# Score blocks of 64 keys, two heads to a fill, and PV in 64x32 tiles, in a fused attention and gated-MLP kernel

## The chip, the cores and the metric

The program runs on one core of a Trainium2 chip. The metric is the device time of one execution in microseconds (us), the median of several runs. TensorE is called PE in the profile, VectorE DVE, ScalarE ACT, GpSimd POOL.

## The reference, cut to what matters

Sequence 2048, width 512, 32 heads of 16, four segments of 512 tokens. Each segment has causal softmax attention within itself (`a_dot`), mixed with a linear-attention memory of the earlier segments (`a_mem`), and a gated MLP runs beside it:

```python
logits = einsum('bhqd,bhkd->bhqk', qs, ks) * scale + mask      # causal, 512 x 512 per head and segment
p = softmax(logits)
a_dot = einsum('bhqk,bhkd->bhqd', p, vs)
...
o = g * a_mem + (1.0 - g) * a_dot                              # then o @ wo
...
gate = gate * (gate > 0)                                       # gate, up: x times 512 x 1792 weights
h = gate * up                                                  # then h @ W_down
...
return g * a + (1 - g) * b                                     # a: attention, b: MLP, g: a gate per token
```

The matter here is the causal triangle. Scores are computed transposed, keys on the partitions and queries along the row. A block of keys needs only the queries from its first key on, so small key blocks waste less of the triangle.

## The kernel before: the parts that matter

One *unit* is 8 heads of one segment (16 units). A *fill* is one use of the score tile `S` (four PSUM banks, 4 x 512 columns): four row groups of TensorE make the scores of four heads at once, ScalarE takes the exponential of all 128 x 2048 into a tile `E`, and GpSimd zeroes the triangle at the diagonal blocks. *PV* then multiplies E by V, four heads side by side in 128x32 tiles. `G` names the other four PSUM banks, one for each other product of TensorE; a bank is free again when ScalarE or VectorE has copied or used its content (an *evacuation*). phi(Q) and phi(K) are the feature maps that the linear-attention memory takes.

```python
# unit(i): 5 fills of 128-key blocks; (key block, head parity, column offset, width)
FL = [[(0, 0, 0, 512)], [(1, 0, 0, 384), (3, 0, 384, 128)], [(2, 0, 0, 256), (2, 1, 256, 256)],
      [(0, 1, 0, 512)], [(1, 1, 0, 384), (3, 1, 384, 128)]]
...
b = op(f"e{s}{c}.{n}", {"ACT": 1.88}, f, deps=[a], ...)                   # exp
for o in offs:                                                            # mask
    v = eb_.t[:, :, o:o + P]
    nc.gpsimd.affine_select(out=v, in_=v, ..., pattern=[[0, 4], [1, P]], channel_multiplier=-1)
m = op(f"m{s}{c}.{n}", {"POOL": 0.7 * len(offs)}, f, deps=[b], ...)
...
# PV of one head parity r, placed behind fill 1 of the next unit
for kb, src, off, w in ((0, ea, 0, 512), (1, ebf, 0, 384), (2, ec, 256 * r, 256), (3, ebf, 384, 128)):
    for j in range(4):
        nc.tensor.matmul(g.t[32 * j:32 * j + 32, L - w:L], lhsT=Vp[s].t[:, kb, h * HP:h * HP + 32],
                         rhs=src.t[:, j, off:off + w], ..., tile_position=(0, 32 * j))
```

Even heads take their 16 rows of K straight from `KT`; odd heads take 32 rows of `KO`, a copy of K with the even heads' rows set to zero (a GpSimd operation).

Everything above is called `op(name, {engine: price}, ...)`. It isn't executed in the order of the source: the kernel has a list scheduler in Python that runs when the program is built. It walks a model of the five engines in which each operation takes its *price* in us, and writes the instructions of each engine in the order that the model found.

The softmax here doesn't subtract the row's maximum and nothing guards it: scores larger than these inputs give would overflow.

Of the kernel before, what the change touches and what calls it, by code (L numbers as in the profile page):

```python
# [8 lines left out]
F32 = mybir.dt.float32  # L9
# [16 lines left out]
VW = H * HP + 16  # L26

# [25 lines left out]
class Sched:  # L53
# [20 lines left out]
    def run(self):  # L74
# [14 lines left out]
        while len(order) < n:  # L89
            best = None  # L90
            for e, lst in cand.items():
                ests = []
                for o in lst:
                    t = max(free[e], o.ready)
                    ok = True
                    for b in o.alloc:
                        fr = b.pool.free
                        if not fr:
                            ok = False
                            break  # L100
                        t = max(t, min(fr)[0])
                    if ok:
                        ests.append((t, o))
                if not ests:
                    continue
                t0 = min(t for t, _ in ests)
                if e == "PE":
                    def pk(x):
                        t, o = x
                        k = o.key  # L110
                        if o.mode == "C":
                            k += 4.0 if mode == "D" else -20.0
                        elif o.mode == "D" and mode == "C" and not o.flex:
                            k += 3.0
                        return (k, o.seq)
                    pick = min((x for x in ests if x[0] <= t0 + 0.02), key=pk)
                else:
                    pick = min((x for x in ests if x[0] <= t0 + 0.02), key=lambda x: (x[1].cls, x[1].key, x[1].seq))
                t, o = pick
                if best is None or (t, o.cls, o.key) < best[0]:  # L120
                    best = ((t, o.cls, o.key), o, e, t)
# [37 lines left out]
def kernel(  # L159
# [36 lines left out]
    mcol = tl("mcol", [P, 1], F32)  # L196
    bdm = tl("bdm", [P, 8, DH], F32)
# [3 lines left out]
    xTp = pool("xT", 3, [P, NC, L])  # L201
    xnp = pool("xn", 1, [P, 4, D])
    hTp = pool("hT", 22, [P, L])
    QTp, KTp, KOp = pool("QT", 6, [P, L]), pool("KT", 6, [P, L]), pool("KO", 6, [P, L])
    pqp = pool("pq", 5, [P, L])
# [3 lines left out]
    Vpp = pool("Vp", 2, [P, 4, VW])  # L209
    Ep = pool("E", 7, [P, 4, L])  # L210
    Tp = pool("T", 3, [P, 2, 16, 32], F32)
# [40 lines left out]
    def c_warm(e):  # L252
        nc.scalar.activation(mcol[:], zero[:, 0:1], ACT.Exp)  # L253
    o_warm = op("warm", {"ACT": 1.5}, c_warm, deps=[o_zero], cls=0, key=-100)

    def c_mcol(e):
        nc.vector.memset(mcol[:], 1.0)
        for j in range(4):
            nc.vector.memset(mcol[32 * j:32 * j + 16, :], 0.0)
    o_mcol = op("mcol", {"DVE": 0.4}, c_mcol, deps=[o_warm], key=-50)  # L260

    def c_vones(e):
        for t in Vpp.tiles:
            nc.gpsimd.memset(t[:].rearrange("p a b -> p (a b)"), 1.0)
    o_vones = op("vones", {"POOL": 4.0}, c_vones, key=-60)
# [217 lines left out]
    o_q, o_k, o_ko, o_pq, o_v = {}, {}, {}, {}, {}  # L483
# [52 lines left out]
    def proj_k(s, c):  # L536
        g, k, ko = Buf(G), Buf(KTp), Buf(KOp)
        KT[s, c], KO[s, c] = k, ko
# [5 lines left out]
        def f(e):  # L544
            (nc.vector if e == "DVE" else nc.gpsimd).tensor_scalar(ko.t[:], k.t[:], mcol[:, 0:1], None, ALU.mult)  # L545
        o_ko[s, c] = op(f"ko{s}{c}", {"DVE": 0.45} if s == 0 and c < 2 else {"POOL": 0.8}, f, deps=[b, o_mcol], key=a.key, cls=1, alloc=[ko], uses=[k])
# [12 lines left out]
    def proj_v(s, t):  # L559
        g = Buf(G)  # L560
        if t == 0:
# [9 lines left out]
                       uses=[g, Vp[s]])  # L571

# [99 lines left out]

    def unit(i):
        s, c = units[i]
        k0 = TA0 + i * PU
        FL = [[(0, 0, 0, 512)], [(1, 0, 0, 384), (3, 0, 384, 128)], [(2, 0, 0, 256), (2, 1, 256, 256)],
              [(0, 1, 0, 512)], [(1, 1, 0, 384), (3, 1, 384, 128)]]
        E, masks = [], []
        for n, parts in enumerate(FL):
            sp, eb_ = Buf(Spool), Buf(Ep)  # L680
            kf = k0 + n * PU / 5

            def f(e, parts=parts, sp=sp):
                for kb, r, off, w in parts:
                    for j in range(4):
                        q0 = L - w
                        if r == 0:
                            rows = slice(32 * j, 32 * j + 16)
                            ks = KT[s, c].t
                        else:  # L690
                            rows = slice(32 * j, 32 * j + 32)
                            ks = KO[s, c].t
                        nc.tensor.matmul(sp.t[:, j, off:off + w], lhsT=ks[rows, kb * P:(kb + 1) * P],  # L693
                                         rhs=QT[s, c].t[rows, q0:L], start=True, stop=True,
                                         tile_position=(32 * j, 0))
            a = op(f"f{s}{c}.{n}", {"PE": MM}, f,
                   deps=[o_q[s, c], o_k[s, c] if all(p[1] == 0 for p in parts) else o_ko[s, c],
                         (fill_prev[0], 0.0) if fill_prev[0] else None],
                   key=kf, mode="R", alloc=[sp], uses=[QT[s, c], KT[s, c], KO[s, c]])
# [10 lines left out]
            def f(e, eb_=eb_, offs=offs):  # L710
                for o in offs:
                    v = eb_.t[:, :, o:o + P]
                    nc.gpsimd.affine_select(out=v, in_=v, compare_op=ALU.is_ge, fill=0.0, base=0,  # L713
                                            pattern=[[0, 4], [1, P]], channel_multiplier=-1)
            m = op(f"m{s}{c}.{n}", {"POOL": 0.7 * len(offs)}, f, deps=[b], key=kf, uses=[eb_])
            E.append(eb_)
            masks.append(m)
        pending[0] = (i, E, masks)
# [5 lines left out]
    def dens(s, k0, org):  # L724
# [12 lines left out]
        def f(e):  # L737
            nc.vector.transpose(T.t[:, 0, :, :].rearrange("p b e -> p (b e)"), g.t[:])
        a = op(f"trd{s}", {"DVE": 0.72}, f, deps=[a], key=k0, cls=0, alloc=[T], uses=[g])

        def f(e):
            nc.gpsimd.tensor_scalar(CMD[:, 0], T.t[:, 0, :, 0:8], 1e-6, None, ALU.add)
# [25 lines left out]
    def rest(i, E, masks, behind):  # L768
        s, c = units[i]
        k0 = TA0 + i * PU  # L770
        pvs = []
        for r in range(2):
            g = Buf(G)
            ea, ebf, ec = E[3 * r], E[3 * r + 1], E[2]

            def f(e, r=r, g=g, ea=ea, ebf=ebf, ec=ec):
                for kb, src, off, w in ((0, ea, 0, 512), (1, ebf, 0, 384), (2, ec, 256 * r, 256), (3, ebf, 384, 128)):
                    for j in range(4):
                        h = 8 * c + 2 * j + r
                        nc.tensor.matmul(g.t[32 * j:32 * j + 32, L - w:L],  # L780
                                         lhsT=Vp[s].t[:, kb, h * HP:h * HP + 32],
                                         rhs=src.t[:, j, off:off + w],
                                         start=(kb == 0), stop=(kb == 3), tile_position=(0, 32 * j))
            a = op(f"pv{s}{c}.{r}", {"PE": 0.57}, f,
                   deps=[masks[3 * r], masks[3 * r + 1], masks[2]] + [o_v[s, t] for t in range(4)] +
                   ([(pvs[0][0], 0.0)] if r else [(behind, 0.0)] if behind else []),
                   key=k0 - 100, mode="C", alloc=[g], uses=[ea, ebf, ec, Vp[s]])
            pvs.append((a, g))
# [19 lines left out]
        for kind, lst in ((0, pvs), (1, recs)):  # L808
            if not lst:
                continue  # L810
            T, O = Buf(Tp), Buf(Op_)
            tr = []
            for r, (a, g) in enumerate(lst):
                def f(e, T=T, g=g, r=r):
                    nc.vector.transpose(T.t[:, r, :, :].rearrange("p b e -> p (b e)"), g.t[:])  # L815
                tr.append(op(f"tr{s}{c}.{kind}{r}", {"DVE": 0.72}, f, deps=[a] + tr, key=k0 + PU * 0.8, cls=0,
                             alloc=[T] if r == 0 else [], uses=[g] + ([] if r == 0 else [T])))
            if kind == 0:
                sm = Buf(smp)

                def f(e, T=T, sm=sm):
                    nc.vector.reciprocal(sm.t[:], T.t[:, :, :, DH])
                    nc.vector.tensor_tensor(sm.t[:], sm.t[:], RG[s % 2][:, c, :, :], ALU.mult)
                a = op(f"cf{s}{c}", {"DVE": 0.55}, f, deps=tr + [org], key=k0 + PU, alloc=[sm], uses=[T])

                def f(e, T=T, sm=sm, O=O):
                    nc.vector.tensor_tensor(O.t[:].rearrange("p b r e -> p r b e"), T.t[:, :, :, 0:DH],
                                            sm.t[:][:, :, :, None].to_broadcast([P, 2, 16, DH]), ALU.mult)
                a = op(f"pr{s}{c}.0", {"DVE": 0.80}, f, deps=[a], key=k0 + PU, alloc=[O], uses=[T, sm])
            else:  # L830
                cm = CM[s]

                def f(e, T=T, cm=cm, O=O):
                    nc.vector.tensor_tensor(O.t[:], T.t[:, 0, :, :].rearrange("p b (r e) -> p b r e", r=2),
                                            cm.t[:, c, :, :, None].to_broadcast([P, 16, 2, DH]), ALU.mult)
                a = op(f"pr{s}{c}.1", {"DVE": 0.80}, f, deps=tr + o_cm[s, c], key=k0 + PU, alloc=[O], uses=[T, cm])
# [4 lines left out]
        deps = [outs[0][0]]  # L841
        if s > 0:
# [4 lines left out]
            deps = [op(f"ad{s}{c}", {"DVE": 0.5} if (s, c) == (NSEG - 1, NC - 1) else {"POOL": 0.8}, f, deps=[outs[0][0], outs[1][0]], key=k0 + PU, uses=[Oa, Ob])]  # L847
# [92 lines left out]
```

## Time and profile before

| | before |
|---|---|
| median | 272.53 us (272.49 to 272.73) |
| TensorE busy | 265.1 of 270.6 us |
| ScalarE, VectorE, GpSimd busy | 209.5, 175.1, 169.0 us |
| granted TensorE clock | 1.00 |

Lines of the page of the kernel before: the busy times, the busy share of GpSimd and the granted clock in 40 equal slices of the span (tenths), and the shares of the chain of waits, followed back from the last instruction.

```profile
PE 265.1 (98%) x2650; PEld 117.2 (43%) x2650; DVE 175.1 (65%) x345; ACT 209.5 (77%) x200; POOL 169.0 (62%) x319
...
POOL 8095889983598892795439963678585352633500
PEclk9999999999999999999999999999999999999999
...
PE 93%; DVE 3%; ACT 1%; ACTq 1%; issue 0%; DVEq 0%
```

The chain is TensorE from end to end, and GpSimd has light slices (2 to 6) between the full ones. The chain in order of time, around the first PV (start in us, length in us, engine, tile, line, matmuls):

```profile
30.84 0.33 PE S L693 x8
31.17 1.20 PE G L780 x32
32.37 1.73 PE G L236 x32
34.10 0.33 PE S L693 x8
34.43 2.70 PE G L238 x12
```

A fill (L693) lasts 0.33 us and streams 512 columns, which at the dense rate is 0.216 us; the other 0.11 us is the change of tiling. PV (L780) is 1.20 us. The dense work behind it (L236, in PV's tiling) runs 8 matmuls' worth of columns in 1.73 us, 0.216 each, with no change of tiling in between. In this profile there are 165 blocks, that is, stretches of matmuls in one tiling.

Two groups of GpSimd (busy us, mean ns of one, idle time before and what ended it):

```profile
L713 POOL TENSOR_SCALAR_AFFINE_SELECT E<-E 128x512 bf16<-128x512 bf16 x128 | 87.5, 703 | 68.0 <-ACT E L706 64.1
L545 POOL TENSOR_SCALAR KO<-KT,mcol 128x512 bf16<-128x512 bf16 x14 | 23.3, 1672 | 9.2 <-ACT KT L503 6.9
```

The masks wait for ScalarE (64.1 us of GpSimd's idle time), so GpSimd is early. Note the 1672 ns of the masked K: the schedule prices it at 0.8 us.

### The profile page before, as it was taken

What the parts mean: (1) busy time and instruction counts of PE and PEld (TensorE: products, weight loads), DVE (VectorE), ACT (ScalarE), POOL (GpSimd) and SP (SyncE); (2) the same over time, 40 slices, a digit from 0 to 9 for tenths busy, and PEclk for the clock granted to TensorE, in tenths of its full rate; (3) what the DMA queues carried; (4) which work ended last, traced back from release to release, by engine and by line L of the source; (5) the groups of instructions that cost most, each with busy time, mean ns of one, the idle gap of its engine ahead of it and who ended that gap; (6) DMA issues with size and microseconds to landing.
All of it is one profiled execution on the core that took longest, in us unless ns stands there. A gap on an engine that the chain in (4) does not pass through costs nothing.

```text
span 270.6 us, 6534 instructions
## 1 busy us (share of the span) xinstructions
PE 265.1 (98%) x2650; PEld 117.2 (43%) x2650; DVE 175.1 (65%) x345; ACT 209.5 (77%) x200; POOL 169.0 (62%) x319
## 2 busy tenths in 40 slices
PE   8999999999999999999999999999999999999995
PEld 6444444434443444434344444343344444434454
DVE  1499978978893454798777543789865432748251
ACT  3599889989977688989996868898878677887511
POOL 8095889983598892795439963678585352633500
PEclk9999999999999999999999999999999999999999
DMA  6998993024400100001001000000000000000002
GB/s 177 282 236 219 321 284 100 0 41 101 95 2 21 41 21 2 0 0 22 19 2 40 33 28 22 1 2 0 2 4 0 22 19 23 20 0 2 2 8 72
DMA packets 27597, 15.49 MB, mean 57 GB/s; under 512 B 13616, under 2 KB 27568, under 8 KB 27568
## 3 DMA queue, kind: packets, MB, share of 16 engines
q1 hardware_dynamic: 26736, 14.63, 21.5%
q10 hardware_dynamic: 832, 0.46, 0.6%
q8 instruction: 20, 0.33, 0.5%
q14 instruction: 9, 0.07, 0.1%
HBM read 9.84 MB, written 2.10 MB: 44 GB/s over the span
## 4 chain that ended last, share of the span: by engine, by line
PE 93%; DVE 3%; ACT 1%; ACTq 1%; issue 0%; DVEq 0%
PE G L238 61%; PE G L236 13%; PE S L693 10%; PE G L780 7%; PE S L396 2%; PE G L578 1%; DVE QT L501 1%; DVE pq L531 1%; DVE pq L530 0%; DVE KT L501 0%; ACT L253 0%; ACT QT L503 0%; PE G L730 0%; ACTq L304 0%; DVE T L815 0%
## 5 line engine op out<-in xcount | busy, mean ns | idle before, releaser
L706 ACT ACTIVATE E<-S 128x2048 bf16<-128x2048 f32 x80 | 150.0, 1875 | 25.5 <-PE S L693 22.0
L713 POOL TENSOR_SCALAR_AFFINE_SELECT E<-E 128x512 bf16<-128x512 bf16 x128 | 87.5, 703 | 68.0 <-ACT E L706 64.1
L618 DVE TENSOR_TENSOR hT<-G,rg 128x512 bf16<-128x512 f32 x56 | 37.6, 679 | 23.0 <-ACT rg L614 17.5
L238 PE MATMUL G<-xT,wu_sb 128*128 128x512 bf16 x194 | 51.0, 380 | 0.0
L238 PE MATMUL G<-xT,wg_sb 128*128 128x512 bf16 x184 | 48.7, 380 | 0.1
L815 DVE STREAM_TRANSPOSE T<-G 128x512 f32<-128x512 f32 x44 | 29.6, 698 | 17.6 <-PE G L780 16.5
L238 PE MATMUL G<-wd_sb,hT 128*128 128x512 bf16 x166 | 40.4, 380 | 0.1
L614 ACT ACTIVATE rg<-G 128x512 bf16<-128x512 f32 x56 | 32.5, 596 | 6.1 <-PE G L236 2.8
L545 POOL TENSOR_SCALAR KO<-KT,mcol 128x512 bf16<-128x512 bf16 x14 | 23.3, 1672 | 9.2 <-ACT KT L503 6.9
L238 PEld LDWEIGHTS <-wu_sb 128*128 128x128 bf16 x194 | 17.7, 98 | 22.6 <-issue 3.5
L238 PEld LDWEIGHTS <-wg_sb 128*128 128x128 bf16 x184 | 16.6, 98 | 21.2 <-issue 4.0
L238 PEld LDWEIGHTS <-hT 128*128 128x128 bf16 x166 | 14.9, 98 | 19.0 <-issue 3.8
L780 PE MATMUL G<-E,Vp 128*32 128x256 bf16 (+3 forms) x512 | 20.5, 301 | 0.0
L657 ACT ACTIVATE os<-G,ngcol 128x512 bf16<-128x512 f32 x11 | 7.6, 687 | 15.2 <-PE G L236 7.5
L850 DVE STREAM_TRANSPOSE oT<-O 128x512 bf16<-128x512 bf16 x16 | 11.3, 705 | 11.8 <-POOL O L846 11.7
L693 PE MATMUL S<-QT,KT 16*128 16x512 bf16 (+3 forms) x256 | 17.3, 302 | 0.1
L693 PE MATMUL S<-QT,KO 32*128 32x256 bf16 (+3 forms) x256 | 17.1, 300 | 0.0
L466 POOL COPY R<-rcol 32x4 f32<-32x4 f32 x64 | 14.7, 229 | 2.6
L780 PEld LDWEIGHTS <-Vp 128*32 128x32 bf16 x512 | 11.4, 96 | 9.3 <-issue 2.7
L238 PE MATMUL G<-xT,wk_sb 128*128 128x512 bf16 x58 | 15.0, 380 | 0.0
L238 PE MATMUL G<-wv_sb,xT 128*128 128x512 bf16 x60 | 14.1, 380 | 0.0
L236 PE MATMUL G<-wd_sb,hT 128*32 128x512 bf16 (+1 forms) x288 | 14.1, 338 | 0.0
(98 smaller groups left out, 316.1 us busy)
## 6 DMA issues: line engine op xcount, KB each, us to landing
out_dram<-os SPq DMA_DIRECT2D x15, 128.0 KB, 1.7
wd_sb<-in_B_W_down_dram SPq DMA_DIRECT2D x1, 1792.0 KB, 12.7
xn<-in_A_x_dram SPq DMA_DIRECT2D x3, 512.0 KB, 4.9
wg_sb<-in_B_W_gate_dram SPq DMA_DIRECT2D x2, 512.0 KB, 5.3
wu_sb<-in_B_W_up_dram SPq DMA_DIRECT2D x2, 512.0 KB, 6.9
wg_sb<-in_B_W_gate_dram SPq DMA_DIRECT2D x3, 256.0 KB, 6.8
wu_sb<-in_B_W_up_dram SPq DMA_DIRECT2D x3, 256.0 KB, 6.6
wk_sb<-in_A_wk_dram SPq DMA_DIRECT2D x1, 512.0 KB, 5.5
```

Source lines behind the costliest of these rows:

```text
L236: nc.tensor.matmul(out_ap[q], lhsT=lhsT[:, q], rhs=rhs, start=start, stop=stop, tile_position=(0, 32 * j))
L238: nc.tensor.matmul(out_ap, lhsT=lhsT, rhs=rhs, start=start, stop=stop)
L466: nc.gpsimd.tensor_copy(R[s][32 * j:32 * j + 32, :, k], rcol[32 * k:32 * k + 32, cols])
L545: (nc.vector if e == "DVE" else nc.gpsimd).tensor_scalar(ko.t[:], k.t[:], mcol[:, 0:1], None, ALU.mult)
L614: nc.scalar.activation(rg.t[:], g.t[:], ACT.Relu)
L618: nc.vector.tensor_tensor(h.t[:], u.t[:], rg.t[:], ALU.mult)
L693: nc.tensor.matmul(sp.t[:, j, off:off + w], lhsT=ks[rows, kb * P:(kb + 1) * P], rhs=QT[s, c].t[rows, q0:L], start=True, stop=True, tile_po ...
L706: nc.scalar.activation(eb_.t[:], sp.t[:], ACT.Exp, scale=SCALE)
L713: nc.gpsimd.affine_select(out=v, in_=v, compare_op=ALU.is_ge, fill=0.0, base=0, pattern=[[0, 4], [1, P]], channel_multiplier=-1)
L780: nc.tensor.matmul(g.t[32 * j:32 * j + 32, L - w:L], lhsT=Vp[s].t[:, kb, h * HP:h * HP + 32], rhs=src.t[:, j, off:off + w], start=(kb == 0 ...
L815: nc.vector.transpose(T.t[:, r, :, :].rearrange("p b e -> p (b e)"), g.t[:])
L850: nc.vector.transpose(dst.t[:], Oa.t[:].rearrange("p b r e -> p (b r e)"))
```

## The change

Intent: key blocks of 64. Two heads of 64 keys share the 128 partitions of a fill, so a fill makes eight heads at a time, the triangle is followed in steps of 64, and a unit needs 4.5 fills (an odd unit's middle block rides in the even unit's fifth fill). PV's contraction is now over 64 rows, so it runs in 64x32 tiles, both head parities at once. Every head now takes 32 rows of K from a doubled copy `K2`, with the other parity's rows zeroed, and half of V is copied to the other half of the partitions (`VS`).

```diff
-        FL = [[(0, 0, 0, 512)], [(1, 0, 0, 384), (3, 0, 384, 128)], [(2, 0, 0, 256), (2, 1, 256, 256)],
-              [(0, 1, 0, 512)], [(1, 1, 0, 384), (3, 1, 384, 128)]]
+        FL = [[(c, 0, 0, 512)], [(c, 1, 0, 448), (c, 7, 448, 64)], [(c, 2, 0, 384), (c, 6, 384, 128)],
+              [(c, 3, 0, 320), (c, 5, 320, 192)]]
+        if not odd:
+            FL.append([(c, 4, 0, 256), (c + 1, 4, 256, 256)])
...                                          # masks
-                for o in offs:
-                    v = eb_.t[:, :, o:o + P]
-                    nc.gpsimd.affine_select(..., pattern=[[0, 4], [1, P]], channel_multiplier=-1)
-            m = op(f"m{s}{c}.{n}", {"POOL": 0.7 * len(offs)}, ...)
+                for off in offs:
+                    for r in range(2):
+                        v = eb_.t[64 * r:64 * r + 64, :, off:off + 64]
+                        nc.gpsimd.affine_select(..., pattern=[[0, 4], [1, 64]], channel_multiplier=-1)
+            m = op(f"m{s}{c}.{n}", {"POOL": 0.8 * len(parts)}, ...)
...                                          # masked K: two instead of one
-        o_ko[s, c] = op(f"ko{s}{c}", {"DVE": 0.45} if s == 0 and c < 2 else {"POOL": 0.8}, ...)
+        for r, mc in ((0, mcole), (1, mcol)):
+            ... tensor_scalar(k2.t[:, :, r, :], k.t[:].rearrange(...), mc[:, 0:1], None, ALU.mult)
+            op(f"k2{s}{c}{r}", {"DVE": 0.45} if r == 0 or (s == 0 and c < 2) else {"POOL": 0.8}, ...)
...                                          # V in the other half of the partitions
+        for r in range(2):
+            nc.gpsimd.tensor_copy(VS[s].t[64 * r:64 * r + 64, t, ...], Vp[s].t[64 - 64 * r:128 - 64 * r, t, ...])
+            op(f"vs{s}{t}{r}", {"POOL": 0.45}, ...)
...                                          # PV: one operation, both parities, a tiling of its own ("P")
+            for kb in range(8):
+                for r in range(2):
+                    for j in range(4):
+                        nc.tensor.matmul(gs[r].t[32 * j:32 * j + 32, L - w:L], lhsT=v, rhs=src.t[rows, j, off:off + w],
+                                         ..., tile_position=(64 * r, 32 * j))
+        a = op(f"pv{s}{c}", {"PE": 1.05}, f, deps=masks + ..., mode="P", alloc=gs, ...)
...                                          # cut: per-parity reciprocals and products, smaller buffer pools
```

## The prediction

> **What bounds the kernel now.** TensorE. The page gives PE 98% busy (265.1 of 270.6 us), ACT 77%, DVE 65%, POOL 62%; the chain of waits is 93% PE. In that chain the work comes in blocks: dense 12 matmuls 2.70 us, a fill of S 0.33 us whether 4 or 8 matmuls, PV of a unit 1.20 us for 32. A fill streams 512 columns: 0.216 us at the dense rate, (2.70-0.11)/12. So each block carries about 0.11 us for its change of tiling. The Trainium skill (TensorEngine Tiling (Array Packing), Key Properties) says that changing the tiling mode drains TensorE; the trace agrees, with 0.11 us each. The starts of the matmuls give some 165 blocks (18 us of changes) around 240 us of streaming; real waits inside are only about 2 us, the worst at 182 us, where segment 3's Q and K come late.
>
> **What the change removes.**
> - 8 of 80 fills: 8 x (0.216 + 0.11 in + 0.11 out) = -3.5 us of PE; also 8 exponentials of 1.875 us = -15 us of ACT, which isn't the bound.
> - PV columns: 2560 to 2304 per unit. Starts of the PV matmuls now span 1.10 us; 0.9 of it is 0.99 us, and with 64 narrower matmuls (issued 3.5 ns apart in the trace) I put it at 1.02: -1.2 us over 16 units.
>
> **What it adds.**
> - PV gets a tiling of its own. Before, the dense work after PV ran in PV's 128x32 tiling at no loss (8 matmuls' columns in 1.73 us = 0.216 each), so leaving PV was free. Now it costs one more change: 16 x 0.11 = +1.8 us. Changes in total stay at about 165.
> - POOL: 256 masks of 64x256 for 128 of 128x512 (703 ns). A line through the 128- and 512-element selects (294, 637 at the median) gives about 410 ns: +19 us; 32 copies of V at about 0.43: +14; a larger memset: +2. POOL 169 to about 204 us (75%).
> - DVE: 16 more masked K at 0.3-0.5, reciprocals and products split in two: 175 to about 184 us.
> - New dependences: the first fill of a unit waited for K alone, now for both masked copies, one a POOL operation of 1.6 us (the program's own schedule counts 0.8). PV takes two G banks at once and needs all masks and copies of V. I allow +1.0 us of new PE waits, mostly at the beginning of segments and in 20 to 80 us, where DVE is at 90%.
>
> **Sum.** -3.5 - 1.2 + 1.8 + 1.0 = -1.9 us: 270.6 us, range 268.6 to 272.8. Faster by over 2%: 0.04; within 2%: 0.91; slower by over 2%: 0.05.
>
> **What would show each step.** 72 fill blocks of 0.33 us; ACT near 195 us; a PV block of 1.1 us (1.02 and a change), followed by dense 128x128 blocks, nearly no dense 128x32 left; blocks still about 165; masks 256 at 0.38-0.45 us; POOL 195-215 us; PE waits on masked K or G banks below 2.5 us in sum.
>
> **What would make it wrong.** (a) Weight loads of 64x32 tiles don't hide under 64- and 128-column steps: PV 1.2 us or more, the gain is nil. (b) The two row halves of a PV step don't stream together: PV near 2 us, +15 us. (c) POOL or DVE is late in 20-80 us: PV or fills wait, several us. (d) PV waits for its second bank, which the schedule's estimate doesn't see, 0.2-0.5 us per unit. (e) The other way: with ACT relieved, evacuations leave DVE, the 2 us of waits disappear: 268 to 269.

## More of the kernel before

On the chip the order of each engine is fixed; only the waits are real.

```python
# Sched.run(), cut: the candidate that could start first, by priority, gets the engine
o.start, o.eng, o.end = t, e, t + o.engs[e]        # o.engs[e] is the price
free[e] = o.end
...
with tc.manual_schedule():
    for o in order:
        o.emit(o.eng)
# dense work after PV may stay in PV's 128x32 tiling, so that no change of tiling is needed:
o.ran = "C" if o.flex and mode == "C" else o.mode
```

## The result

| | before | changed |
|---|---|---|
| median | 272.63 us (272.49 to 273.16) | 284.47 us (284.45 to 286.63) |
| ratio, 95% interval | | 1.0459 (1.0406 to 1.0511) |
| TensorE, ScalarE, VectorE, GpSimd busy | 265.1, 209.5, 175.1, 169.0 | 265.1, 194.0, 179.7, 210.7 us |
| granted clock | 1.00 | 0.974 to 0.993 |

Slower by 4.6%: +11.8 us between the medians, where the prediction had -1.9 us. Ratios here and below are the mean time of one kernel's fast runs over that of the other's of the same rounds, so they are not quite the ratio of the medians quoted.

The page of the changed kernel, the same lines:

```profile
PE 265.1 (93%) x2626; PEld 119.0 (42%) x2661; DVE 179.7 (63%) x402; ACT 194.0 (68%) x188; POOL 210.7 (74%) x481
...
POOL 9299889989889886799858988648988886636000
PEclk9999999997999999999899997999999999999999
...
PE 58%; POOL 27%; issue 6%; DVE 5%; ACT 3%; POOLq 0%; DVEq 0%; ACTq 0%
```

GpSimd is at 8 or 9 tenths in most slices, and it holds 27% of the chain, from nothing ("issue" is time in which the profile shows nothing to wait for). Yet on average it is busy only 74% of the span, less than ScalarE was before. The average didn't show the danger.

The blocks of TensorE are as predicted. (Its busy time did not fall, 265.1 us, though e1 below has 258.3 with the same matmuls: the profiled execution is the one of 286.63 us, and in it TensorE ran for three stretches of 3.41 us at half the clock, from 65.08, 140.17 and 174.30 us, which is up to 5 us of longer matmuls.) The chain in order of time shows PV in its new tiling, and then the place where the first large wait lies:

```profile
45.40 0.33 PE S L716 x8
45.73 1.10 PE G L818 x64
46.83 0.16 issue
46.99 1.67 PE G L242 x7
...
61.20 0.36 PE S L716 x8
61.56 0.02 issue
61.58 1.88 ACT E L730
63.46 0.49 ACT rg L637
63.95 0.53 ACT etk L532
64.47 0.06 issue
64.53 0.41 POOL E L738
```

PV takes 1.10 us with its change of tiling, the predicted 1.1, and dense 128x128 work follows. (The page lists 2626 matmuls for 2661 weight loads, so some records are missing, and the 0.16 us of "issue" after this PV holds one.) The matmuls of one PV step start 2 to 5 ns apart, and the steps follow each other at the rate of their columns, from 227 ns for 512 to 56 ns for 128, with no pause before the last of 64; so the weight loads are hidden. Risks (a) and (b) of the prediction did not come.

At 61.56 the chain leaves TensorE for 3.9 us. TensorE in that stretch, the timeline of TensorE alone (start, length, instruction, count, and in brackets how long the engine was idle and what ended it):

```profile
61.13 0.40 PE L716 MATMUL S<-QT,K 32*128 32x448 bf16 x8
...
62.05 0.31 PE L818 MATMUL G<-E,Vp 64*32 64x320 bf16 x4
64.99 0.37 PE L818 MATMUL G<-E,Vp 64*32 64x256 bf16 x4 [2.64 <-POOL E L738]
...
66.12 0.61 PE L242 MATMUL G<-xT,wu_sb 128*128 128x512 bf16 x1
66.95 0.63 PE L242 MATMUL G<-xT,wu_sb 128*128 128x512 bf16 x1 [0.22 <-issue]
```

PV begins, comes to a block whose mask isn't done, and TensorE stands for 2.64 us in the middle of it. There was dense work to do, but it lies behind PV in the fixed order. The chain above names ScalarE for 2.9 of the 3.9 us, and that is misleading. Counted off against the schedule's plan, the select at 64.53 belongs to a fill whose exponential had ended at 56.97 us and whose mask was planned for 57.79: GpSimd came to it 6.7 us late, with no pause of more than 0.07 us since 57.94. And the wait has an echo: the windows table of the changed kernel over the same place (busy time of each engine, then the granted clock):

```profile
core 0: us, PE busy (x) PEld busy (x) DVE busy (x) ACT busy (x) POOL busy (x), PEclk, DMA share, GB/s
61.10:62.05 0.95, 0.95 (x38) 0.51 (x41) 0.85 (x4) 0.47 (x1) 0.89 (x2) 1.00 0.22 43
62.05:64.99 2.94, 0.30 (x18) 0.08 (x1) 0.32 (x1) 2.41 (x3) 2.48 (x9) 1.00 0.22 45
64.99:66.10 1.11, 1.00 (x32) 0.60 (x31) 0.00 (x0) 0.00 (x0) 0.98 (x3) 0.54 0.00 0
66.10:68.40 2.30, 2.08 (x19) 0.57 (x12) 2.04 (x4) 0.00 (x0) 2.06 (x5) 0.50 0.00 0
```

GpSimd is busy throughout (2.48 of 2.94 us), and after the wait the granted clock is half for 3.4 us. The Trainium skill (TensorE: Matmul & The Clock Gate, Why this matters for your kernels) says to leave no idle gap of over about 3 us, or the clock falls to half; here a gap of 2.64 us was followed by a clock of 0.50. The runs give no sharp limit: in the profiled runs of the control c1, a gap of 2.63 us at the same place, and of b11, one of 2.89 us, were not followed by a lower clock, and the half-clock stretch at 174.30 us here has no gap over 0.95 us in the 3 us before it. Mean clocks of 0.988 to 0.993 in most runs of the changed kernel put this echo at some 2 to 3 us of the time (estimate: 0.010 of 283 us). The two runs at 286.6 and 286.9 us are the ones with 0.982 and 0.974.

Further on the chain is GpSimd's instructions one after another. From the chain in order of time:

```profile
93.07 0.41 POOL E L738
93.54 0.41 POOL E L738
94.02 0.41 POOL E L738
```

Each select lasts 0.41 us but the next starts 0.47 us after it. A pair, which the schedule prices at 0.8 us, takes 0.95. The groups:

```profile
L738 POOL TENSOR_SCALAR_AFFINE_SELECT E<-E 64x256 bf16<-64x256 bf16 x256 | 115.9, 453 | 30.9 <-ACT E L730 16.8
L553 POOL TENSOR_SCALAR K<-KT,mcol 128x512 bf16<-128x512 bf16 x14 | 22.2, 1591 | 6.0 <-ACT KT L509 5.1
L589 POOL COPY VS<-Vp 64x256 bf16<-64x256 bf16 x32 | 14.0, 438 | 1.6
```

The masks' wait for ScalarE fell from 64.1 to 16.8 us: GpSimd is now the late one of the two.

The waits for masks inside PV are only a part. From the table of waits (us in total, times, longest), and from the chain in order of time:

```profile
PE G L818 <- POOL E L738: 4.0, 4, 2.6
DVE oT L899 <- POOL O L895: 18.4, 10, 3.4
...
137.23 1.16 POOL O L895
139.05 0.66 DVE hT L641
139.75 0.64 PE G L242 x2
```

TensorE's gaps of over 0.05 us sum to 15.4 us (4.1 in e1), and four waits in PV are 4.0 of them. The others of over 0.4 us all end with an instruction of VectorE. At 139.75 a dense product had waited 1.99 us for VectorE's product `hT`. VectorE's order is fixed too: just before it stands a transpose that waited 3.44 us for GpSimd's sum of the two outputs (`O`, 137.23). Another such wait, 1.0 us at 106.35, follows GpSimd's sum at 103.70 in the chain. So late GpSimd work reaches TensorE on two paths: through the masks, and through VectorE.

The plan of the schedule can be set beside this, since it gives each operation a start. It planned 183.5 us of GpSimd work and an end at 268.3 us; measured are 210.7 us busy. (Busy time leaves out the pauses between instructions; with the measured prices of e4 below, which count them, the same work is 226.8 us of plan.) For the kernel before it planned 154.1 us (measured 169.0) and an end at 271.2 us. How far the first select of a fill starts behind its plan:

```text
                      planned start of the mask, us:  17    36    54    73    91   111   131   150   170   189   209   228
changed kernel, lag in us:                            0.2   2.5   5.8   6.3   9.4  6.9   9.9  13.1  14.4  17.4  18.0  16.6
kernel before, lag in us (plans from 17 to 253 us):   never above 1.8, and mostly about -1 from 107 us on
```

So there are two statements to separate. GpSimd has more to do (load). And the order of all engines was made for a GpSimd that is faster than the real one (order).

### The profile page after: what moved, and what is told of

It reads as the page before. It is cut to its first block, busy times and chain, and to the rows that moved or that the text cites. A ratio compares the mean times of both kernels' runs of the same rounds, so it can differ in the third digit from the quotient of the medians.

```text
span 284.9 us, 6734 instructions
## 1 busy us (share of the span) xinstructions
PE 265.1 (93%) x2626; PEld 119.0 (42%) x2661; DVE 179.7 (63%) x402; ACT 194.0 (68%) x188; POOL 210.7 (74%) x481
## 4 chain that ended last, share of the span: by engine, by line
PE 58%; POOL 27%; issue 6%; DVE 5%; ACT 3%; POOLq 0%; DVEq 0%; ACTq 0%
PE G L242 44%; POOL E L738 12%; PE S L716 5%; PE G L818 4%; POOL R L472 3%; POOL CM L792 3%; POOL K L553 2%; POOL O L895 2%; ACT E L730 2%; PE G L240 2%; PE S L402 1%; POOL M L618 1%; DVE T L853 1%; PE G L285 1%; DVE hT L641 1%
## 5 line engine op out<-in xcount | busy, mean ns | idle before, releaser
L730 ACT ACTIVATE E<-S 128x2048 bf16<-128x2048 f32 x72 | 135.0, 1875 | 48.7 <-PE S L716 44.6
L738 POOL TENSOR_SCALAR_AFFINE_SELECT E<-E 64x256 bf16<-64x256 bf16 x256 | 115.9, 453 | 30.9 <-ACT E L730 16.8
L242 PE MATMUL G<-wd_sb,hT 128*128 128x512 bf16 (+1 forms) x231 | 54.6, 373 | 0.8 <-issue 0.6
L716 PE MATMUL S<-QT,K 32*128 32x192 bf16 (+7 forms) x512 | 29.0, 291 | 0.8
L553 POOL TENSOR_SCALAR K<-KT,mcol 128x512 bf16<-128x512 bf16 x14 | 22.2, 1591 | 6.0 <-ACT KT L509 5.1
L818 PE MATMUL G<-E,Vp 64*32 64x128 bf16 (+7 forms) x512 | 21.0, 299 | 3.2 <-POOL E L738 3.0
L818 PE MATMUL G<-E,VS 64*32 64x64 bf16 (+7 forms) x512 | 20.7, 298 | 1.1 <-POOL E L738 1.0
L242 PE MATMUL G<-wo_sb,oT 128*128 128x512 bf16 (+1 forms) x66 | 16.8, 366 | 0.2 <-issue 0.2
L818 PEld LDWEIGHTS <-Vp 64*32 64x32 bf16 x512 | 12.6, 95 | 10.1 <-issue 7.2
L895 POOL TENSOR_TENSOR O<-O,O 128x512 bf16<-128x512 bf16 x11 | 12.8, 1161 | 4.6 <-DVE O L873 4.0
```

Of the source, the lines that this page charges most:

```text
L242: nc.tensor.matmul(out_ap, lhsT=lhsT, rhs=rhs, start=start, stop=stop)
L553: (nc.vector if e == "DVE" else nc.gpsimd).tensor_scalar(k2.t[:, :, r, :], k.t[:].rearrange("p (b k) -> p b k", k=64), mc[:, 0:1], None, A ...
L716: nc.tensor.matmul(sp.t[:, j, off:off + w], lhsT=K2[s, cc].t[rows, kb, :, :].rearrange("p r k -> p (r k)"), rhs=QT[s, cc].t[rows, L - w:L] ...
L730: nc.scalar.activation(eb_.t[:], sp.t[:], ACT.Exp, scale=SCALE)
L738: nc.gpsimd.affine_select(out=v, in_=v, compare_op=ALU.is_ge, fill=0.0, base=0, pattern=[[0, 4], [1, 64]], channel_multiplier=-1)
L818: nc.tensor.matmul(gs[r].t[32 * j:32 * j + 32, L - w:L], lhsT=v, rhs=src.t[rows, j, off:off + w], start=(kb == 0), stop=(kb == 7), tile_po ...
```

## The experiments

Theory 1: TensorE waits because GpSimd is late, either by load or by order (theory 2 later: by wrong prices). Rival A: the new dependences do it, PV's two banks at once and the fills' wait for both masked K. In the table the median of each kernel stands beside that of the kernel before on the same chip; "busy" is GpSimd's.

| run | median us | before us | ratio (95%) | GpSimd busy us |
|---|---|---|---|---|
| changed kernel | 284.47 | 272.63 | 1.0459 (1.0406-1.0511) | 210.7 |
| e1 one select for two | 268.42 | 272.75 | 0.9845 (0.9816-0.9875) | 152.3 |
| e2 no copies of V | 275.66 | 272.75 | 1.0113 (1.0085-1.0141) | 196.2 |
| e3 before, masks split | 273.58 | 272.75 | 1.0062 (1.0003-1.0121) | 186.7 |
| e4 all prices measured | 274.37 | 272.75 | 1.0062 (1.0036-1.0087) | 210.4 |
| e5 mask price alone | 280.53 | 272.86 | 1.0285 (1.0244-1.0326) | 210.4 |
| e5b all but the mask price | 280.30 | 272.96 | 1.0275 (1.0254-1.0296) | 210.5 |
| e6 before, prices measured | 272.60 | 272.86 | 0.9986 (0.9953-1.0019) | 168.3 |
| e7 before, PV's tiling alone | 274.05 | 272.96 | 1.0044 (1.0028-1.0060) | 167.8 |
| c1 control | 282.97 | 272.87 | 1.0364 (1.0327-1.0401) | 209.6 |
| c3 two banks | 283.51 | 272.87 | 1.0401 (1.0360-1.0443) | 209.7 |
| b3 product, either engine | 272.12 | 272.86 | 0.9963 (0.9930-0.9995) | 139.0 |
| b5 product on GpSimd | 273.29 | 272.86 | 1.0009 (0.9978-1.0040) | 161.5 |
| b6 the same, V copies back | 271.43 | 272.96 | 0.9947 (0.9921-0.9973) | 178.5 |
| b7 either engine, V copies back | 272.58 | 272.96 | 0.9994 (0.9978-1.0010) | 161.2 |
| b8 masked K on ScalarE | 269.12 | 272.87 | 0.9857 (0.9832-0.9883) | 187.5 |
| b8 and two banks | 269.28 | 272.87 | 0.9861 (0.9835-0.9886) | 187.6 |
| b10 before, b8's mends | 272.22 | 273.24 | 0.9967 (0.9952-0.9981) | 144.6 |
| b11 b8 with the old prices | 276.45 | 273.24 | 1.0127 (1.0110-1.0143) | 186.7 |

One more version was built that cut both blocks of a fill in one select; it didn't compile and was not run.

### e1: half of the selects, same order (wrong result)

```diff
-                    for r in range(2):
-                        v = eb_.t[64 * r:64 * r + 64, :, off:off + 64]   # base=0
+                    v = eb_.t[:, :, off:off + 64]                        # base=64
```

> The changed kernel, same order of everything, but the two 64-partition selects of each masked block are one select of 128 partitions by 256 elements with an offset of 64 (wrong result on purpose: the even heads leak future keys). GpSimd loses 128 selects, about 60 us of its 211. Theory 1 (TensorE waits because GpSimd is late): most of the 12 us come back, 269 to 271 us, granted clock back to 1.00, GpSimd share of the chain from 27% to under 5%. Rival A (PV takes two G banks at once and the fills wait for both masked K, neither of which this touches): stays above 279 us.

Measured 268.42 us, a little below the range. The page of this run:

```profile
PE 258.3 (97%) x2626; PEld 117.6 (44%) x2661; DVE 179.7 (67%) x402; ACT 193.6 (73%) x188; POOL 152.3 (57%) x353
...
PE 90%; DVE 3%; ACT 3%; issue 2%; DVEq 0%; ACTq 0%
```

GpSimd is out of the chain. Everything that Rival A names is still there, and the time is 4.3 us under that of the kernel before, so Rival A falls. It also measures the TensorE side of the change: -4.3 us where the prediction had -2.9 before its allowance for waits. One caution: the plan still holds a slot for the selects that are gone, so this run lightens GpSimd and loosens the plan at the same time.

### e2: no copies of V, same order (wrong result)

```diff
-                nc.gpsimd.tensor_copy(VS[s].t[...], src[:, :, r, 0:DH])
+                pass
```

> The changed kernel, same order, without the 32 copies of V into the swapped halves (wrong result on purpose). GpSimd loses 14 us of 211. Theory 1: the time falls in proportion to the GpSimd work that came on top, by 2 to 5 us, to 280 to 282 us. Rival A: within 1 us of 284.5. If the masks alone are the cause (Theory 1b) under 1.5 us.

Measured 275.66 us: 8.8 us for 14 us of GpSimd work, where I expected 2 to 5. The expectation was too linear. Some 2 to 3 of the 8.8 us are the slow clock, which these runs don't have (0.999 to 1.0). As in e1 the slots stay in the plan, so the 14 us are also slack for all later GpSimd work.

### e3: the kernel before with the changed kernel's number of selects

```diff
-                    v = eb_.t[:, :, o:o + P]                       # pattern [[0, 4], [1, P]]
+                    for jj in (0, 2):
+                        v = eb_.t[:, jj:jj + 2, o:o + P]           # pattern [[0, 2], [1, P]]
```

> The kernel before with each 128x512 select cut into two of 128x256 (two heads each), correct result. GpSimd gets the changed kernel's mask work, about +28 us to 197, and nothing else of the change. Theory 1: the kernel before gets slower too, 276 to 281 us, with GpSimd in its chain. Rival A: stays within 1.5 us of 272.6.

Measured 273.58 us, +0.8 us at the median (0.1 to 3.3 us by the ratio's interval), and a miss for Theory 1 as I had put it. The page:

```profile
PE 260.9 (96%) x2617; PEld 117.0 (43%) x2650; DVE 169.6 (62%) x345; ACT 209.6 (77%) x200; POOL 186.7 (69%) x447
...
PE 77%; POOL 14%; issue 3%; ACT 2%; DVE 2%; POOLq 0%; DVEq 0%
```

GpSimd enters the chain, but its masks fall at most 4.5 us behind plan and catch up again. The split masks alone, in the structure of before, cost little. But the dose is smaller than the number of selects says: with 128 partitions the next select of a row starts 0.36 us after the last one at the median, a little before that one ends, and in the changed kernel, with 64 partitions and as many elements, 0.48 us after it. So e3 has the changed kernel's number of selects, not their time.

### e4: measured prices, same instructions

```diff
-            m = op(f"m{s}{c}.{n}", {"POOL": 0.8 * len(parts)}, ...)
+            m = op(f"m{s}{c}.{n}", {"POOL": 0.96 * len(parts)}, ...)
```
and likewise masked K 0.8 to 1.62, the sum of outputs 0.8 to 1.2, row copies 0.8 to 1.0, the `cm` copies 0.9 to 1.1, two small ones of the denominators.

> The changed kernel with the instructions unchanged, but its list schedule told the measured GpSimd times (a pair of selects 0.96 for 0.8, masked K 1.62 for 0.8, the sum of outputs 1.2 for 0.8, row copies 1.0 for 0.8, and so on). Theory 1 in the form 'the fixed order is wrong' (order): 276 us or below. Theory 1 in the form 'GpSimd is short of time whatever the order' (capacity): 281 us or above.

Measured 274.37 us, with GpSimd as busy as in the changed kernel:

```profile
PE 260.0 (95%) x2604; PEld 117.3 (43%) x2640; DVE 183.1 (67%) x406; ACT 191.5 (70%) x184; POOL 210.4 (77%) x481
...
PE 66%; POOL 18%; DVE 4%; issue 4%; DMA 3%; ACT 3%; SPq 0%; POOLq 0%; DVEq 0%; ACTq 0%
```

(A few evacuations went from ScalarE to VectorE, where the schedule may choose; GpSimd has the same 481 instructions.) Of the 16 us between e1 and the changed kernel, 10 come back with the order alone, by the same estimate 2 to 3 of them because the clock stays at 0.999 to 1.0. The largest lag of a mask behind plan falls from 18.9 to 4.7 us. The planned end hardly moves (268.3 to 269.0 us), so an order that fits the real GpSimd better was there to be found; the wrong prices led to another one.

### e5 and e5b: which prices

> The changed kernel, instructions unchanged, but its list schedule is told only the measured price of the masks: 0.96 us for a pair of 64x256 selects in place of 0.8. Telling it all GpSimd prices gave 274.4 us. Theory 2 (the change's own underpriced masks put the fixed order wrong): 274 to 277 us, nearly all of that gain. Rival B (the prices inherited from the kernel before, masked K 0.8 for 1.6, sums 0.8 for 1.16, row copies, are what breaks now): 280 us or more.

> The changed kernel, instructions unchanged, its list schedule told all measured GpSimd prices except that of the masks (left at 0.8 for the measured 0.96 a pair). The other corner of the square: none 284.5, masks alone 280.5, all 274.4. If the two errors add: 278 to 279 us. If the inherited prices are the main part and the masks' error matters only on top of them: 275 to 277 us. If both must be right together: above 281 us.

The square: no price measured 284.5, the masks' alone 280.5, all the others 280.3, all of them 274.4 us. My theory that the change's own underpriced masks were nearly everything fell; each half gives about 4 us, both together 10. (The clock is 0.994 to 1.0 in both, so by the estimate above 2 to 3 us of each 4 are slow clock that stayed away; what is left of each half, 1 to 2 us, is no more than the control below shows.) The largest lags are 12.8 and 12.3 us against 18.9 and 4.7. The other prices were inherited from the kernel before.

### e6: measured prices in the kernel before

> The kernel before with the measured GpSimd prices in its list schedule, instructions unchanged. Theory 2 says that wrong prices cost nothing where GpSimd has slack (169 of 271 us): 271 to 273.5 us, same as before within 0.5%. If it falls by over 2 us the kernel before was losing to its prices too, and the comparison of before and after was never about the change alone.

Measured 272.60 us, ratio 0.9986: as expected, nothing. The same wrong prices cost nothing where GpSimd has slack.

### c1 and c3: control, and the two banks

c1 shifts prices that have nothing to do with GpSimd (relu 0.62 to 0.60, transposes 0.72 to 0.70, PV 1.05 to 1.0). c3 repairs the schedule's estimate for an operation that takes two buffers of one pool:

```diff
-                        t = max(t, min(fr)[0])
+                        t = max(t, fr[n_][0])          # the n_-th free one, for the n_-th asked for
```

> Control. The changed kernel with the same instructions, its schedule's prices shifted by 0.02 to 0.05 us for the relu, the transposes and PV, nothing of GpSimd; its order moves in places. If wrong GpSimd prices are the cause: 282 to 287 us. If any reshuffling gives some gain by chance: outside that, e.g. under 280.

> The changed kernel with one repair in its schedule: an operation that takes two G banks starts no earlier than the second bank is free. The prediction's risk (d). If that risk was real: 2 to 6 us less than 284.5, since PV no longer blocks TensorE for its second bank. If it wasn't: 282 to 287, like the control.

282.97 and 283.51 us: another order isn't enough by itself, and the prediction's risk (d) costs at most about a microsecond. The control moves by 1.5 us, which is a fair measure of what reshuffling does. The 10 us of e4 are well outside it. The 4 us of e5 and e5b are outside it only with the clock's share: at full clock c1's profiled run took 282.12 us, those of e5 and e5b 280.44 and 280.33.

### e7: the change of tiling behind PV, in the kernel before

```diff
-                o.ran = "C" if o.flex and mode == "C" else o.mode
+                o.ran = o.mode
```

> The kernel before, except that no dense product is run in PV's 128x32 tiling: after PV TensorE must go back to 128x128, as it must in the changed kernel. This is the prediction's term for leaving PV alone: 16 changes of tiling of 0.11 us, +1.8 us, 274.0 to 275.0 us. If leaving PV costs nothing: within 0.5 us of 272.7. If the 128x32 products were slower than they looked: a gain.

Measured 274.05 us at the median and +0.44% in the ratio, which is 1.2 us, for 20 more blocks in the trace (185 for 165). The sign holds. Twenty changes of 0.11 us would be 2.2 us, so each cost about 0.06 here; but the order moved as well (planned end 272.9 for 271.2 us), so the run doesn't measure a change of tiling by itself.

### b3, b5, b6, b7: masks as products

All use the measured prices and mask with a product by a tile of zeros and ones, both blocks of a fill in one instruction:

```diff
+                (nc.vector if e == "DVE" else nc.gpsimd).tensor_tensor(v, v, m_, ALU.mult)   # 128 x 4 x 2 x 64
```

b3 lets the schedule choose the engine, b5 puts all on GpSimd; both move V's copies to ScalarE. b6 and b7 leave those on GpSimd.

> A mended version, correct result: mask as a product with a 128x64 tile of zeros and ones, both blocks of a fill in one instruction, on VectorE or GpSimd as the schedule finds; V copies on ScalarE; measured GpSimd prices. GpSimd falls to about 150 us, VectorE rises to about 195. Theory 2 with the PE sum measured by the one-select run (268.4): 268.5 to 271 us. If VectorE becomes the late engine: above 272.

> As the other mended version, but the mask products all on GpSimd (72 of about 0.7 to 1.2 us for 256 selects of 0.45), V copies on ScalarE, measured prices. GpSimd about 175 us. Theory 2: 268.5 to 271 us. If the two-input product on GpSimd is slower than 1.25 us for 512 elements, up to 274.

> Mended version, correct result: mask as one product for both blocks of a fill on GpSimd, V copies left on GpSimd, measured prices; unlike the earlier mended one nothing is moved to ScalarE, which had pushed evacuations onto VectorE (195 us). GpSimd about 175 us, VectorE about 182. If the late VectorE is what kept the two mended versions from 268.4: 269 to 271 us. If GpSimd at 175 us is still late: 272 to 274.

> As the last one, but the schedule may put a mask product on VectorE or GpSimd. GpSimd about 150 us, VectorE about 188. 269 to 271 us if each of the two engines under about 190 us leaves TensorE free; 271.5 or more if VectorE's load between 20 and 80 us is what makes TensorE wait.

272.12, 273.29, 271.43 and 272.58 us: correct, level with the kernel before or up to 0.5% faster, and above the 268.4 us I was aiming at: all four lie above the range that their expectations hoped for, which ended at 271 us. b6 has GpSimd at 178.5 us, but VectorE went up from 183.1 us (e4) to 194.2 with the same 406 instructions:

```profile
PE 258.6 (95%) x2626; PEld 117.9 (44%) x2661; DVE 194.2 (72%) x406; ACT 191.9 (71%) x184; POOL 178.5 (66%) x300
...
PE 65%; DVE 21%; DMA 7%; issue 4%; ACT 1%; SPq 0%; DVEq 0%
```

The product that makes phi(K) on VectorE takes 728 ns on average in b6 and 472 ns in e4. The mean hides two groups: eight of the twelve take 424 to 548 ns, as all do in e4 (424 to 551), and four take 1257 to 1327 ns; during those four GpSimd was in an instruction with two inputs, three mask products and one sum of outputs. The Trainium skill (Advanced Engine Details and Errata, Miscellaneous Facts) says that GpSimd shares a read and a write interface with VectorE and conflicts with VectorE instructions that have two inputs in SBUF; these numbers agree with it, though no run here isolates the interface. A saving on one engine came out as a cost on the next.

### b8: the second masked K on ScalarE

```diff
-                (nc.vector if e == "DVE" else nc.gpsimd).tensor_scalar(k2..., mc[:, 0:1], None, ALU.mult)
+                if e == "ACT":
+                    nc.scalar.activation(k2.t[:, :, r, :], src, ACT.Copy, scale=mc[:, 0:1])
```
with e4's prices. ScalarE is the engine that the change relieved. `b8_two_banks` adds c3's repair.

> Mended version, correct result: measured GpSimd prices, and the second masked K (14 of 1.6 us on GpSimd) made by ScalarE as a copy scaled per partition, about 0.62 us each. GpSimd falls from 210 to about 188 us, VectorE stays near 183. If GpSimd's load is what keeps 274.4 from 268.4: 270 to 272 us. If it is the order alone: 273 to 275.

> As the last one, with the repair of the two banks as well. Within 1 us of it if the banks don't matter; 1 to 2 us less if they do.

269.12 us, ratio 0.9857, correct: the best correct kernel, 1.4% faster than the kernel before and 5% faster than the change as it was given. The repair adds nothing (269.28). The page of b8:

```profile
PE 262.0 (98%) x2598; PEld 117.2 (44%) x2598; DVE 183.5 (69%) x404; ACT 200.5 (75%) x200; POOL 187.5 (70%) x467
...
PE 92%; DMA 5%; DVE 1%; SPq 0%; issue 0%; DVEq 0%
```

The chain is TensorE again, GpSimd has no share in it, and no mask is over 0.6 us behind plan. Its PV, from the chain in order of time, is the predicted block without a gap:

```profile
44.14 0.33 PE S L719 x8
44.47 1.10 PE G L821 x64
45.58 1.83 PE G L242 x8
```

b8 does two things at once: it takes 23 us from GpSimd, and a fill gets its masked K from a step of 0.72 us (14 of them on ScalarE) instead of 1.6. Which of the two gives the 5 us over e4 was not separated.

### b10 and b11: whose gain, and do prices still matter

> The kernel before with its masked K on ScalarE and measured GpSimd prices, as in the mended version, without the change. TensorE bounds it and GpSimd is not late: 271.5 to 273.5 us. If the mends themselves make the gain: 270 us or less.

> The mended version (269.1 us) with the schedule's old GpSimd prices: masks 0.8 a pair, sums 0.8, row copies 0.8. GpSimd about 188 us as there. If wrong prices cost only where GpSimd has no slack: 270 to 273 us. If the order they give is bad at any load: 275 us or more.

b10: 272.22 us; the mends give the kernel before 0.3%. The 1.4% of b8 is therefore mostly the change's. b11: 276.45 us, 7 us above b8, where I gave 270 to 273 to the view that prices matter only without slack. At a GpSimd load of 68 to 70% of the span, wrong prices still cost this program 7 us; at 62%, in e6, they cost the kernel before nothing. Against the changed kernel, with the same old prices, b11 gains 8.0 us by the masked K alone.

## Why the prediction was wrong

- *TensorE bounds the kernel; fills 0.33 us, changes of tiling 0.11 us.* Right. 164 blocks after, 165 before.
- *8 fills fewer, PV 1.02 us and a change.* Right: PV 1.10 us with its change. With GpSimd's part out of the way (e1) the whole change gives -4.3 us; the sum without waits was -2.9.
- *+1.8 us for leaving PV's tiling.* Right in sign; e7 has +1.2 us, for 20 changes and another order.
- *GpSimd 204 us, masks about 410 ns, ScalarE near 195, VectorE 184.* Right: 210.7 us, 413 ns at the median (453 on average), 194.0 and 179.7. Not in it: the pause after each select of 64 partitions (starts 0.48 us apart), which busy time doesn't count.
- *"I allow +1.0 us of new PE waits."* This is the step that failed. Measured it is 16 us: 284.47 for the changed kernel against 268.42 for e1, of which 2 to 3 us are the slow clock after the waits. The prediction named late GpSimd as risk (c), "several us", gave it no weight in the sum, and looked for it between 20 and 80 us because VectorE is full there. It came everywhere: by the windows table TensorE of the changed kernel is idle 4.0, 3.5, 2.8, 2.1 and 2.4 us in the five stretches of 40 us from 40 to 240 us, where before it was 0.5 us at most.
- *Risk (d), the second bank.* Did not come: c3 is within a microsecond.

The error had a form worth naming. The prediction treated GpSimd as an engine with an average load of 75% and slack to spare. But its place in the program is fixed by a plan, and the prediction had seen that the plan prices the masked K at half its real length. It did not do the sum that follows: 183.5 us planned, 204 predicted, so the plan is short by 20 us (27 by the measured busy time, 43 by the measured prices), and GpSimd falls behind its plan all through the run, by 18.9 us at most. TensorE then waits in the middle of PV, or for VectorE that waits for GpSimd, with dense work ready behind. Ten of the 16 us go with the order alone (e4); of the other six, b8 recovers five, by a shorter masked K and less load. Taken the other way round the shares differ: the masked K first gives 8.0 us (b11), the prices after it 7.3.

Open: why the kernel before stands the same error. e3 has 186.7 us of GpSimd work on a plan of 154.1, by busy time an even larger shortfall, and loses 0.8 us; b11 has 186.7 on 172.3 and loses 7 us against b8. The plans show one difference: in the kernel before the last mask that a PV needs is planned to end 8.3 us (first half) and 2.8 us (second half) before that PV, at the median, and in the changed kernel 1.8 us, so a late mask reaches TensorE sooner. The changed kernel makes all of PV wait for all masks of a unit and for V's copies, where before each half waited for its own; that is a possible reason, and no run tests it. Nor was it tested whether the smaller buffer pools matter; e1 has them and reaches 268.4 us.

## What to carry to other kernels

When a program's order is fixed by a model, a change is judged against that model too: add up the model's prices for each engine before and after, and set them beside measured times. An engine at 74% that is underpriced can hold the chain where one at 77% (ScalarE before) doesn't. Before tuning such a change away, re-price and re-order it: here the same instructions went from 284.5 to 274.4 us, and one operation moved to the engine that the change had relieved made it 269.1 us.

## What the Trainium skill lacked or had wrong

- TensorEngine Tiling (Array Packing), Key Properties, says that a change of tiling drains TensorE, without a figure. Here each costs 0.11 us between a fill, PV and dense work, in either direction, worked out from the lengths of the blocks; the 20 changes that e7 added cost 0.06 us each, in another order.
- TensorE: Matmul & The Clock Gate, Why this matters for your kernels, puts the gap to avoid at about 3 us. Here 2.64 us without a matmul was followed by a granted clock of 0.50 for 3.41 us, but 2.63 us (c1) and 2.89 us (b11) were not; the runs show no sharp limit.
- GPSIMD Engine Reference, Performance versus the Vector engine, gives a ratio of 1.96, for a sum of two fp32 tiles of 2048 elements. For the masked K, one bf16 tile of 512 elements, it was 3.6 (1591 ns on GpSimd, 447 ns on VectorE, means of the changed kernel), and ScalarE made it in 717 ns as a scaled copy.
- No page that I read has the cost of a select by shape: 64 partitions x 256 elements took 453 ns, 128 x 256 (e3) 447 ns and 128 x 512 took 703 ns on average, so half of the elements saved a third and half of the partitions nothing. Nor does a page have the pause: in a row, selects of 128 x 256 start 0.36 us apart, those of 64 x 256 0.48 us (medians of e3 and the changed kernel).
